# Windowed attention and a three-way maxout layer on one core: the small global transposes are written into the value products' banks

## The chip, the cores and the metric

The kernel runs on one core of a Trainium2 chip. The metric is device time in microseconds (us), from a median of several runs. TensorE (PE in the profile) does the matrix products and writes to PSUM, a memory of eight banks of 128 partitions by 2 KiB (512 numbers of 4 bytes per partition); VectorE (DVE) and ScalarE (ACT) read PSUM and write SBUF; GpSimd (POOL) works in SBUF; SyncE (SP) issues the DMAs.

## The reference

For each of 8 batches and 8 heads there are 512 local and 32 global positions of width 64. A local query sees the 32 global keys and the local keys at a distance of at most 32; a global query sees all keys. The outputs of all heads make a row of 512 numbers for each of the 8 x 544 positions, and each row goes through `max(x@w1, x@w2, x@w3) @ w_out` with widths 512, 768 and 512.

```python
s_ll = np.where(np.abs(pos[:, None] - pos[None, :]) <= 32, scale * q_l @ k_l.T, -1e9)
a_l = sm(np.concatenate([scale * q_l @ k_g.T, s_ll], axis=-1))
out_l = a_l @ np.concatenate([v_g, v_l])
out_g = sm(scale * q_g @ k_all.T) @ v_all
h = np.maximum(np.maximum(x @ w1, x @ w2), x @ w3)
out = h @ w_out
```

## The kernel before

Two heads of a batch make a pair `p` (32 of them). The 512 local queries of a pair are cut in four blocks of 128, and `sl = 4 * p + t` counts these blocks: 128 passes of one loop, called slots here. For each slot:

- `scores(sl)`: products of queries and a window of 192 or 224 keys into an S bank (L313 in the first 28 slots, L317 later; a `pm` bank in the first 12), reduction for the maximum on VectorE (L320), exponential on ScalarE (L322), the reciprocal of the sums (L324, L325) and the scaling (L112). The result goes by DMA into `early` or `prob`.
- `trans(sl)`: four transposes on TensorE into the T bank (L340), copied to the tile `pt`.
- `transg(sl)`: one transpose of 128x128 (L361) of a part of `probg`, which holds the global queries' probabilities. Its result is copied to the columns 128 to 160 of `pt` (hi by `copy`, L102 or L100; the rest by `sub`, L94).
- `pv(sl)`: the product of values and `pt` (L381 in slots 0 to 25, L388 later) into the tile O of two banks, of which it uses columns 0 to 160 of the first bank (early) or 0 to 320 of both (later). Later slots read O four times: a copy of its lower half (lox, L102 or L100), an addition of halves (L394) and two more additions (L396) that give `xr`. Early slots read it once, by a copy to `xr`.
- `glob(p, step)`: the global queries' scores into an S bank (L271, later L275), reduced in L279, for the next pair in the slots with t = 0 and 1; `glob_soft` (L287 to L293) follows with t = 2 and moves the result by six DMAs (L296) to `probg`.

From slot 26 on the operands are split in a rounded part and a rest of it (`copy` and `sub`); `copy`, `sub` and `times` choose their engine by a running sum of costs per engine. The maxout layer of the batch before is a generator of matmuls into `pm` banks (L419 and L438, 512 columns each); `fill(n)` takes n of them and so lays them between the parts of a slot: 18 per slot. In the first part of the program the layer's weights are loaded and converted (L160 to L180) by `weight_step`.

PSUM is used up: three `pm` banks, two for S, one for T, two for O. O is there once, S twice, so an allocation of S waits until the tile two allocations before has been read. The program is written in the order of the loop; a scheduler then sets each engine's order by its own costs and adds the semaphore waits, so the order on an engine is fixed when the kernel is built.

Of the kernel before, what the change touches and what calls it, by code (L numbers as in the profile page):

```python
# [9 lines left out]
F32 = mybir.dt.float32  # L10
# [37 lines left out]
def f32(ap):  # L48
    return ap.bitcast(F32)


def body(ctx, tc, kin, qin, vin, min_, w1, w2, w3, w4, out):
# [8 lines left out]
    psS = ctx.enter_context(tc.tile_pool(name="psS", bufs=2, space=PSUM))  # L61
    psT = ctx.enter_context(tc.tile_pool(name="psT", bufs=1, space=PSUM))
    psO = ctx.enter_context(tc.tile_pool(name="psO", bufs=1, space=PSUM))
# [12 lines left out]
    def spend(e, ns):  # L76
        load[e] += ns
# [11 lines left out]
    def sub(out, a, b, psum=False):  # L89
        n = width(out)  # L90
        c = {"d": n * 1.04 + (160 if psum else 110)}
        if not psum:
            c["p"] = n * 2.32 + 130
        (dve if least(c) == "d" else pool).tensor_tensor(out=out, in0=a, in1=b, op=ALU.subtract)  # L94

    def copy(out, a, psum=False):
        n = width(out)
        c = {"d": n * (1.04 if psum else 0.52) + (160 if psum else 150), "a": n * 0.833 + (150 if psum else 190)}
        if least(c) == "d":
            dve.tensor_copy(out=out, in_=a)  # L100
        else:
            act.copy(out=out, in_=a)  # L102
# [229 lines left out]
    def trans(sl):  # L332
# [15 lines left out]
        else:  # L348
# [2 lines left out]
            copy(v[:, :, 0, 0:128], src, True)  # L351
            sub(v[:, :, 1, 0:128], src, f32(v)[:, :, 0, 0:128], True)

    def transg(sl):
        if sl >= NS:
            return
        p, t = divmod(sl, 4)
        pt = pts[sl]
        i, h, n = GCH[t]
        g = psS.tile([128, 512], F32, name="S")  # L360
        pe.transpose(g.bitcast(F32R)[:, 0:128], probg[p % 2][:, i], identr)  # L361
        src = g[:, 64 * h:64 * h + 64 * n].rearrange("p (c j g) -> p c j g", j=2, g=SG)
        if sl < NAT:
            copy(pt.rearrange("p j c q -> p c j q")[:, 0:n, :, 128:160], src, True)
            return
        v = pt.rearrange("p j c a q -> p c j a q")
        hi, lo = v[:, 0:n, :, 0, 128:160], v[:, 0:n, :, 1, 128:160]
        copy(hi, src, True)
        sub(lo, src, f32(hi), True)

    def pv(sl):
        p, t = divmod(sl, 4)
        pt = pts.pop(sl)
        o = psO.tile([128, 2, 512], F32, name="O")
        if t == 0:
            xr[p] = xp.tile([128, 4, 160], F32, name="xr")
        if sl < NAT:

            for c, j in ((0, 0), (0, 1), (1, 0), (1, 1)):
                n = 160 if c < GCH[t][2] else 128  # L380
                pe.matmul(o[64 * j:64 * j + 64, 0, 0:n], lhsT=vraw[sl][:, 2 * j + c], rhs=pt[:, j, c, 0:n], start=(c == 0), stop=(c == 1))  # L381
            copy(xr[p][:, t], o[:, 0, 0:160], True)
        else:

            for j in range(2):
                for c in range(2):
                    n = 160 if c < GCH[t][2] else 128
                    pe.matmul(o[:, j, 0:320].rearrange("p (a q) -> p a q", a=2)[:, :, 0:n],  # L388
                              lhsT=vs[sl][:, 2 * j + c].rearrange("p a d -> p (a d)"),
                              rhs=pt[:, j, c, :, 0:n], start=(c == 0), stop=(c == 1))  # L390
            lo = att.tile([64, 2, 160], F32, name="lox", bufs=1)
            copy(lo, o[64:128, :, 0:160], True)
            spend("d", 460 + 2 * 320)
            dve.tensor_tensor(out=lo, in0=o[0:64, :, 160:320], in1=lo, op=ALU.add)  # L394
            for j in range(2):
                dve.tensor_tensor(out=xr[p][64 * j:64 * j + 64, t], in0=o[0:64, j, 0:160], in1=lo[:, j], op=ALU.add)  # L396
        if t == 3:
            dve.tensor_reduce(out=xg[:, p % NP, p // NP], in_=xr[p][:, :, 128:160].rearrange("p t g -> p g t"),
                              axis=AX.X, op=ALU.add)
# [101 lines left out]
    load_v(2)  # L501
    weight_load()
    transg(0)
    for sl in range(NS):
        p, t = divmod(sl, 4)
        b, n = divmod(p, NP)
        settle(4500)
        if sl % 16 == 0 and b:
            fill(400)
            mm[0] = moe_local(b - 1)  # L510
        trans(sl + 1)
        fill(4)
        next_scores(max(min(sl + 5, EARLY - 1), sl + 3))
        if t == 2:
            split_k(p + 2)
            load_k(p + 3)
        fill(4)
        pv(sl)
        if t <= 1:
            glob(p + 1, t)  # L520
        elif t == 2:
            glob_soft(p + 1)
        fill(3)
        transg(sl + 1)
        fill(7)
        split_v(sl + 2)
        load_v(sl + 3)
        for _ in range(WS[sl] if sl < len(WS) else 0):
            weight_step()
        if sl % 16 >= 12:  # L530
            i = sl % 16 - 12
            q = b * NP + i
            xs.setdefault(b, []).append(split_x(xr[q][:, :, 0:128], SL))
# [56 lines left out]
```

## Time and profile before

| | |
|---|---|
| time, median of 3 runs | 861.93 us (860.92 to 863.58) |
| time of the profiled execution | 862.75 us |
| its span, first to last instruction | 860.8 us |
| TensorE busy / weight loads | 809.9 / 673.8 us |
| VectorE, ScalarE, GpSimd busy | 577.0, 517.2, 509.9 us |
| granted TensorE clock, mean | 0.977 |
| L361 transposes | 128, median 222 ns |

In rows of the trace the first number is the start in us and the second the duration; `x4` counts merged instructions, and the brackets give idle time of the engine before the row and what ended it. In rows of waits the numbers are total us, times, and the longest. "Behind" a value product means after the end of its last matmul.

### The profile page before, as it was taken

The page shows a single profiled execution, that of the slowest core. Times are in us where ns is not written, and L with a number is a line of the kernel's source. Part 1 is how long each engine was busy: PE and PEld are TensorE (multiplying, and loading weights), DVE is VectorE, ACT ScalarE, POOL GpSimd, SP SyncE. Part 2 cuts the span into 40 slices and gives each one's busy share as a digit, 9 for nine tenths or more (in the row PEclk, how much of TensorE's full clock was granted, in tenths as well). Part 3 has the DMA queues.
Part 4 walks back from the last instruction along what each step waited for, and adds up shares of the span by engine and source line. Part 5 has one row for each costly group of instructions (what it writes and reads, how often), then busy time and mean ns, then how long its engine had stood idle before and what let it go on. Part 6 is the DMA issues. An engine that isn't in the chain of part 4 may idle for free.

```text
span 860.8 us, 15729 instructions
## 1 busy us (share of the span) xinstructions
PE 809.9 (94%) x4452; PEld 673.8 (78%) x4452; DVE 577.0 (67%) x1806; ACT 517.2 (60%) x1457; POOL 509.9 (59%) x683
## 2 busy tenths in 40 slices
PE   5857888899999999999999999999999999999997
PEld 3534565688888888888888888888888888888896
DVE  5567999677777677776777777867787776511111
ACT  4654554587677667767777777776777776511111
POOL 4535676686667666776768576766677664411211
PEclk8886999999999999999999999999999999999999
DMA  6685664435333533344333533353334322100001
GB/s 211 188 245 162 195 197 146 137 95 156 99 106 102 160 112 107 99 126 127 100 110 100 150 98 103 92 163 108 111 112 131 123 79 67 62 24 1 26 25 25
DMA packets 107238, 98.53 MB, mean 114 GB/s; under 512 B 21008, under 2 KB 97936, under 8 KB 107152
## 3 DMA queue, kind: packets, MB, share of 16 engines
q1 hardware_dynamic: 107152, 97.53, 37.5%
q8 instruction: 36, 0.59, 0.3%
q14 instruction: 50, 0.41, 0.1%
HBM read 56.85 MB, written 8.91 MB: 76 GB/s over the span
## 4 chain that ended last, share of the span: by engine, by line
PE 83%; DVE 7%; DMA 5%; SPq 2%; issue 2%; ACT 1%; POOL 1%; DVEq 0%; ACTq 0%; POOLq 0%
PE pm L419 46%; PE pm L438 17%; PE O L388 7%; PE S L317 5%; PE T L340 4%; DVE wraw L170 2%; PE S L275 1%; DMA wraw<-w_in 1%; DMA probg<-sg 1%; DMA prob<-s 1%; DVE cut L171 1%; PE S L361 1%; PE pm L313 1%; SPq L296 1%; DMA early<-s 1%
## 5 line engine op out<-in xcount | busy, mean ns | idle before, releaser
L419 PE MATMUL pm<-xs,wh 128*128 128x512 f32 (+1 forms) x1296 | 408.9, 389 | 1.4 <-POOL xs L94 0.9
L419 PEld LDWEIGHTS pm<-xs,wh 128*128 128x128 f32 x1296 | 234.1, 190 | 34.3 <-POOL xs L94 1.2
L419 PE MATMUL pm<-xs,wl 128*128 128x512 f32 (+1 forms) x648 | 253.5, 391 | 0.0
L112 POOL TENSOR_SCALAR s<-s,z 128x192 f32<-128x192 f32 (+1 forms) x249 | 113.4, 468 | 86.4 <-ACT lox L102 36.8
L322 ACT ACTIVATE s<-s,nm 128x192 f32<-128x192 f32 (+1 forms) x256 | 118.1, 462 | 40.1 <-DVE nm L320 35.3
L419 PEld LDWEIGHTS pm<-xs,wl 128*128 128x128 f32 x648 | 122.9, 190 | 22.5 <-issue 1.8
L438 PE MATMUL pm<-woh,h 128*128 128x512 f32 x408 | 133.5, 398 | 0.0
L94 POOL TENSOR_TENSOR h<-m,h 128x512 fp32r<-128x512 f32 (+1 forms) x54 | 67.5, 1250 | 96.2 <-ACT h L102 96.1
L427 DVE TENSOR_TENSOR m<-pm,m 128x512 f32<-128x512 f32 (+1 forms) x108 | 71.1, 658 | 71.7 <-PE pm L419 71.4
L94 POOL TENSOR_TENSOR qs<-qraw,qs 128x256 fp32r<-128x256 f32 x100 | 73.9, 749 | 54.9 <-ACT qs L102 41.2
L94 DVE TENSOR_TENSOR pt<-T,pt 128x512 fp32r<-128x512 f32 x102 | 70.5, 691 | 49.3 <-ACT pt L102 47.4
L324 DVE TENSOR_SCALAR z<-z 128x2 f32<-128x2 f32 x128 | 55.0, 430 | 50.9 <-ACT s L322 50.2
L320 DVE CUSTOM_DVE_ANT_0 s<-S,mask 128x192 f32<-128x192 f32 (+1 forms) x232 | 78.1, 370 | 11.9 <-PE S L313 5.6
L438 PEld LDWEIGHTS pm<-woh,h 128*128 128x128 f32 x408 | 74.7, 188 | 11.5
L438 PE MATMUL pm<-wol,h 128*128 128x512 f32 x204 | 81.8, 401 | 0.0
L94 POOL TENSOR_TENSOR vs<-vraw,vs 128x256 fp32r<-128x256 f32 x102 | 75.6, 741 | 10.0 <-ACT vs L102 6.5
L94 POOL TENSOR_TENSOR kst<-kraw,kst 64x576 fp32r<-64x576 f32 x50 | 71.9, 1439 | 11.8 <-issue 8.3
L102 ACT CAST pt<-T 128x512 fp32r<-128x512 f32 x91 | 53.2, 585 | 40.2 <-PE T L340 39.9
L388 PEld LDWEIGHTS O<-pt,vs 128*128 128x128 f32 x408 | 66.5, 188 | 9.1
L388 PE MATMUL O<-pt,vs 128*128 128x320 f32 (+1 forms) x408 | 72.8, 300 | 0.0
L102 ACT CAST qs<-qraw 128x256 fp32r<-128x256 f32 x100 | 40.7, 407 | 49.8 <-PE S L317 48.1
L340 PEld LDWEIGHTS T<-identr,prob 128*128 128x128 f32 x448 | 50.3, 141 | 22.3 <-ACT s L322 2.6
(93 smaller groups left out, 1282.4 us busy)
## 6 DMA issues: line engine op xcount, KB each, us to landing
vraw<-v_in SPq DMA_DIRECT2D x128, 128.0 KB, 2.5
qraw<-q_in SPq DMA_DIRECT2D x100, 128.0 KB, 2.2
prob<-s SPq DMA_DIRECT2D x56, 224.0 KB, 2.4
prob<-s SPq DMA_DIRECT2D x56, 192.0 KB, 2.3
wraw<-w_in SPq DMA_DIRECT2D x18, 512.0 KB, 5.1
out_dram<-o SPq DMA_DIRECT2D x32, 256.0 KB, 2.5
kraw<-k_in SPq DMA_DIRECT2D x25, 320.0 KB, 3.1
qn<-q_in SPq DMA_DIRECT2D x28, 128.0 KB, 3.7
```

What stands on the lines that cost most here:

```text
L94: (dve if least(c) == "d" else pool).tensor_tensor(out=out, in0=a, in1=b, op=ALU.subtract)
L102: act.copy(out=out, in_=a)
L112: pool.tensor_scalar(out=out, in0=a, scalar1=col, scalar2=1.0, op0=ALU.mult, op1=ALU.mult)
L317: pe.matmul(ph[j][:, 0:n], lhsT=qs[sl][:, a, 128 * j:128 * j + 128], rhs=kst[p][:, j, c0:c0 + n], start=(a == 0), stop=(a == 1))
L320: dve.tensor_tensor_reduce(out=s[:, j, 0:n], in0=ph[j][:, 0:n], in1=mask[:, (1, 0, 1, 0)[t], 32 * (t == 0):32 * (t == 0) + n], scale=-0.12 ...
L322: act.activation(out=s[:, j, 0:n], in_=s[:, j, 0:n], func=AF.Exp, bias=nm[:, j:j + 1], scale=-1.0, accum_out=z[:, j:j + 1])
L324: dve.tensor_scalar(out=z, in0=z, scalar1=1e-9, scalar2=None, op0=ALU.add)
L340: i = pe.transpose(pr[:, 256 * j + 128 * c:256 * j + 128 * c + 128], s[:, j, 128 * c:128 * c + 128], identr)
L388: pe.matmul(o[:, j, 0:320].rearrange("p (a q) -> p a q", a=2)[:, :, 0:n], lhsT=vs[sl][:, 2 * j + c].rearrange("p a d -> p (a d)"), rhs=pt[ ...
L419: pe.matmul(ps[:, 0:n], lhsT=w[f][:, i, k], rhs=xs[k][:, a, 0:n], start=(q == 0), stop=(q == 11))
L427: dve.tensor_tensor(out=m[:, 0:n], in0=ps[:, 0:n], in1=m[:, 0:n], op=ALU.max)
L438: pe.matmul(ps, lhsT=hh[f][:, a, 128 * t:128 * t + 128], rhs=w[:, f], start=(q == 0), stop=(q == 17))
```

## The change

`transg` no longer allocates an S tile. It writes its 128 columns into columns 384 to 512 of the second bank of the O tile that the last `pv` used (a first one is allocated for slot 0). `pv` puts its new tile in the list `obank`. The S banks are left to `scores` and `glob`. Line numbers behind `transg` rise by 5: L361 becomes L366, L388 L393, L394 L399, L396 L401, L419 L424.

```diff
+    obank = [None]
+
     def transg(sl):
...
         i, h, n = GCH[t]
-        g = psS.tile([128, 512], F32, name="S")
+
+        if obank[0] is None:
+            obank[0] = psO.tile([128, 2, 512], F32, name="O")
+        g = obank[0][:, 1, 384:512]
         pe.transpose(g.bitcast(F32R)[:, 0:128], probg[p % 2][:, i], identr)
...
     def pv(sl):
         p, t = divmod(sl, 4)
         pt = pts.pop(sl)
-        o = psO.tile([128, 2, 512], F32, name="O")
+        o = obank[0] = psO.tile([128, 2, 512], F32, name="O")
```

TensorE in a slot with t = 0 in the middle of the program, before, from the last value product on (`pm` rows are fillers, the numbers behind names tell tiles apart):

```order
L388 MATMUL O_6215<-pt_6104,vs_6091 128x2x128
L275 MATMUL S_6229<-kst_6042,qgz_96 128x384 [waits PE_49]
L275 MATMUL S_6229<-kst_6042,qgz_96 128x384
L419 MATMUL pm_6184<-xs_6096,wl0_108 128x512
L419 MATMUL pm_6184<-xs_6171,wh0_102 128x512 [waits Activation_49]
L419 MATMUL pm_6184<-xs_6171,wh0_102 128x512 [waits Pool_49]
L361 MATMUL S_6237<-identr_87,probg0_94 128x128 [waits DMAHW3_49,DMAHW2_49,DVE_49]
L419 MATMUL pm_6184<-xs_6171,wl0_108 128x512
```

The same place after:

```order
L393 MATMUL O_6135<-pt_6025,vs_6012 128x2x128
L275 MATMUL S_6149<-kst_5964,qgz_96 128x384 x2
L424 MATMUL pm_6104<-xs_6017,wl0_108 128x512
L424 MATMUL pm_6104<-xs_6091,wh0_102 128x512
L424 MATMUL pm_6104<-xs_6091,wh0_102 128x512 [waits Pool_49]
L424 MATMUL pm_6104<-xs_6091,wl0_108 128x512
L424 MATMUL pm_6162<-xs_5846,wh0_102 128x512 x2
L424 MATMUL pm_6162<-xs_5846,wl0_108 128x512
L366 MATMUL O_6135<-identr_87,probg0_94 128x128 [waits DMAHW2_49,DMAHW3_49,DVE_49,Activation_49]
```

The transpose stood behind three fillers and waited for VectorE's reading of an S tile. It stands behind seven now, writes the tile of the value product just ahead of it (O_6135), and waits for VectorE and ScalarE; the score product L275 has lost its wait. The VectorE instruction that it waits for is the second L401 of that tile. With t = 2 and 3, where no L275 is in between, it comes behind eight fillers. No filler is added or dropped.

VectorE in the next slot (t = 1), before, from the addition on O:

```order
L394 TENSOR_TENSOR lox_6300<-O_6295,lox_6300 64x320 [waits Activation_49]
L279 ISA sg_6226,nmg_6227<-S_6305,sg_6226 64x160 [waits Activation_49]
L279 ISA nmg_6227 64x1
L396 TENSOR_TENSOR xr_6216<-O_6295,lox_6300 64x160 [waits DVE_49]
L396 TENSOR_TENSOR xr_6216<-O_6295,lox_6300 64x160
L94 TENSOR_TENSOR pt_6260<-S_6313,pt_6260 128x2x32 [waits Activation_49]
L287 TENSOR_TENSOR nmg_6227<-nmg_6227 64x1 [waits DVE_49]
L427 TENSOR_TENSOR m_6183<-pm_6292,m_6183 128x512 [waits PE_49]
```

The same place after:

```order
L399 TENSOR_TENSOR lox_6219<-O_6214,lox_6219 64x320 [waits Activation_49]
L279 ISA sg_6146,nmg_6147<-S_6224,sg_6146 64x160 [waits Activation_49]
L279 ISA nmg_6147 64x1
L401 TENSOR_TENSOR xr_6136<-O_6214,lox_6219 64x160 [waits DVE_49]
L401 TENSOR_TENSOR xr_6136<-O_6214,lox_6219 64x160
L287 TENSOR_TENSOR nmg_6147<-nmg_6147 64x1 [waits DVE_49]
L289 TENSOR_SCALAR zg_6148<-zg_6148 64x1 [waits Activation_49]
L94 TENSOR_TENSOR pt_6179<-O_6214,pt_6179 128x2x32 [waits Activation_49]
L432 TENSOR_TENSOR m_6103<-pm_6211,m_6103 128x512 [waits PE_49]
```

The subtraction that reads the transposed block (`pt` from S, now from O) went behind L287, and L289, which waits for ScalarE's exponential, now stands ahead of it and of the maximum (L427, now L432). The additions on O and the reduction L279 between them keep their places.

TensorE near the program's start, before, from the second slot's transposes on:

```order
L340 MATMUL T_242<-identr_87,early_114 128x128 [waits DMAHW2_49,Activation_49]
L340 MATMUL T_242<-identr_87,early_114 128x128 x3
L361 MATMUL S_239<-identr_87,probg0_94 128x128 [waits DMAHW6_49,DMAHW3_49]
L271 MATMUL S_293<-kn_130 64x384
L381 MATMUL O_283<-pt_233,vraw_128 64x160 [waits Activation_49]
L381 MATMUL O_283<-pt_233,vraw_128 64x160
L381 MATMUL O_283<-pt_233,vraw_128 64x128 x2
L361 MATMUL S_296<-identr_87,probg0_94 128x128 [waits DMAHW5_49,DMAHW4_49,PE_49]
```

After, from the third slot's scores on:

```order
L313 MATMUL pm_190<-kn_118,qn_126 128x224 [waits DMAHW4_49]
L313 MATMUL pm_190<-kn_118,qn_126 128x224
L271 MATMUL S_293<-kn_130 64x384 [waits DMAHW6_49,DVE_49]
L313 MATMUL pm_207<-kn_118,qn_132 128x192 [waits DMAHW7_49,DVE_49]
L313 MATMUL pm_207<-kn_118,qn_132 128x192
L313 MATMUL pm_249<-kn_130,qn_149 128x192 [waits DMAHW0_49,DVE_49]
L313 MATMUL pm_249<-kn_130,qn_149 128x192
L313 MATMUL pm_266<-kn_130,qn_166 128x224 [waits DMAHW1_49,DVE_49]
```

The second pair's first global scores (S_293) stood behind the first transpose of `probg`; they now stand ahead of the scores of the fourth slot.

## The prediction

> **What bounds the kernel now.** I read the page's engine line and its slices first, then busy time by stage, then who TensorE waits for, and last the single slots (a slot is one pass of the loop over `sl`).
>
> ```profile
> span 860.8 us, 15729 instructions
> PE 809.9 (94%) x4452; PEld 673.8 (78%) x4452; DVE 577.0 (67%) x1806; ACT 517.2 (60%) x1457; POOL 509.9 (59%) x683
> PE   5857888899999999999999999999999999999997
> ```
>
> TensorE is the bound as a whole, with two regimes: partly idle in the first eight slices (about 170 us), full after that.
>
> ```profile
> core 0: us, PE busy (x) PEld busy (x) DVE busy (x) ACT busy (x) POOL busy (x), PEclk, DMA share, GB/s
> 80.00:100.00 20.00, 15.19 (x86) 10.65 (x87) 19.82 (x54) 10.64 (x33) 13.94 (x12) 1.00 0.68 199
> 120.00:140.00 20.00, 17.36 (x90) 12.53 (x91) 19.76 (x41) 11.15 (x29) 13.48 (x14) 0.95 0.67 194
> 400.00:500.00 100.00, 100.00 (x555) 84.85 (x554) 74.96 (x244) 71.45 (x201) 69.20 (x97) 1.00 0.38 114
> ...
> PE S L361 <- DMA probg<-sg: 14.1, 4, 4.4
> PE S L361 <- DVE nm L320: 6.2, 5, 2.2
> ...
> PE S L361 <- DVE nm L320: 2.2, 1, 2.2
> PE T L340 <- DMA prob<-s: 0.4, 1, 0.4
> ```
>
> The windows show VectorE as the early limit from 80 to 140 us (19.8 of 20) and a TensorE without any idle time from 200 us on (100.00 of 100). The first two wait rows are of the whole run; the last two are all that TensorE waits for between 165 and 760 us. So what the change takes away, the global transpose's (L361) wait for a score bank still being read (released by L320), is 6.2 us in five waits, and only 2.2 us of it lies in the full stretch. In that stretch every new wait of TensorE goes straight onto the end: the filling matmuls are issued in a fixed order behind it.
>
> **The change part by part.** The same instructions run on every engine; only the bank of 128 transposes and the order move.
>
> *Removed: waits for an S bank.* At most 6.2 us; surely on the path is the single 2.2 us at the start of the full stretch. The others lie where VectorE or DMAs set the pace. I take 3 us.
>
> *Moved early: the global scores.* In the new order the second pair's global scores (L271) stand before its local scores and no longer behind the first global transpose. They are two short matmuls beside idle TensorE time. VectorE's reduction that follows stands at nearly its old place, and the four waits for `probg` (14.1 us) hang on the DMAs behind it. I take nothing; the ends are -14.1 us (all go) and +5 us (shuffled weight conversions on the VectorE-bound stretch, about the 6.2 us row turned round).
>
> *Added: the transpose waits for the value product's readers.* From slot 26 on, `pv` leaves two banks that are read by a copy (lox), L394 and twice L396. The transpose of the next slot now writes into the second of these banks, and the new program makes it wait for the second L396. To cover this wait the scheduler put the transpose 8 filling matmuls behind `pv` (7 and the global scores where t is 0 or 1), where before it came after 3. Is that far enough? One slot of each t, first TensorE's rows, then VectorE's:
>
> ```profile
> 496.09 0.69 PE L388 MATMUL O<-pt,vs 128*128 128x320 f32 x4
> 497.31 0.22 PE L361 MATMUL S<-identr,probg 128*128 128x128 f32 x1
> 498.06 0.65 DVE L396 TENSOR_TENSOR xr<-O,lox 64x160 f32<-64x160 f32 x2
> ...
> 501.68 0.74 PE L388 MATMUL O<-pt,vs 128*128 128x320 f32 x4
> 502.96 0.22 PE L361 MATMUL S<-identr,probg 128*128 128x128 f32 x1
> 503.54 0.23 DVE L94 TENSOR_TENSOR pt<-S,pt 128x64 fp32r<-128x64 f32 x1
> 503.68 0.64 DVE L396 TENSOR_TENSOR xr<-O,lox 64x160 f32<-64x160 f32 x2
> ...
> 507.35 0.69 PE L388 MATMUL O<-pt,vs 128*128 128x320 f32 x4
> 508.23 0.40 PE L419 MATMUL pm<-xs,wl 128*128 128x512 f32 x1
> 508.46 0.62 PE L419 MATMUL pm<-xs,wh 128*128 128x512 f32 x2
> 508.92 0.22 PE L361 MATMUL S<-identr,probg 128*128 128x128 f32 x1
> 508.98 0.45 PE L419 MATMUL pm<-xs,wl 128*128 128x512 f32 x1
> 509.26 0.63 PE L419 MATMUL pm<-xs,wh 128*128 128x512 f32 x2
> 509.89 0.65 DVE L396 TENSOR_TENSOR xr<-O,lox 64x160 f32<-64x160 f32 x2
> ...
> 513.32 0.74 PE L388 MATMUL O<-pt,vs 128*128 128x320 f32 x4
> 514.82 0.22 PE L361 MATMUL S<-identr,probg 128*128 128x128 f32 x1
> 515.30 0.64 DVE L396 TENSOR_TENSOR xr<-O,lox 64x160 f32<-64x160 f32 x2
> ```
>
> Filling matmuls start 0.23 us apart (508.23, 508.46). So the transpose's new place is its old start plus 5 x 0.23 = 1.15 us in the first two slots (t = 2, 3) and plus 4 x 0.23 = 0.92 us in the others (t = 0, 1): 498.46, 504.11, 509.84, 515.74. The second L396 ends at 498.71, 504.32, 510.54, 515.94: later in all four. In the second slot the subtraction `pt<-S` (L94) stood ahead of L396 and took 0.14 us of its time (503.54 to 503.68); it now comes behind, so 504.18 there.
>
> What a late release costs TensorE is seen where a transpose did wait for VectorE:
>
> ```profile
> 133.87 0.08 DVE L320 DVE_READ_ACCUMULATOR2_ANT nm<- 128x1 f32 x1
> 134.01 0.14 PEld L361 LDWEIGHTS S<-identr,probg 128*128 128x128 f32 x1 [2.17 <-DVE nm L320]
> 134.12 0.46 PE L419 MATMUL pm<-xs,wl 128*128 128x512 f32 x1
> 134.42 0.62 PE L419 MATMUL pm<-xs,wh 128*128 128x512 f32 x2
> ```
>
> The release is at 133.95, the second matmul behind the transpose starts at 134.42, 0.47 us later; without a wait (508.92 to 509.26) it is 0.34 us behind the transpose's own start. The delay is therefore release minus place plus 0.13 us: 0.38 (t=2), 0.20 (t=3), 0.83 (t=0), 0.33 (t=1), together 1.74 us in four slots. There are 101 such transposes, about 25 sets of four: 43.5 us as the upper bound.
>
> The lower bound asks how early the readers can be done if nothing is queued before them:
>
> ```profile
> L396 DVE TENSOR_TENSOR xr<-O,lox x204: 303/317/320, 175.9 to 755.8; 64x160 f32<-64x160 f32 x102
> L394 DVE TENSOR_TENSOR lox<-O,lox x102: 460/481/485, 175.4 to 754.9; 64x320 f32<-64x320 f32 x102
> L102 ACT COPY lox<-O x97: 422/423/425, 174.6 to 754.5; 64x320 f32<-64x320 f32 x97
> ```
>
> 0.42 + 0.48 + 2 x 0.32 = 1.54 us, with three or four handovers of 0.03 about 1.65 us behind the end of `pv`. The place lies 1.68 us behind it (498.46 less the 496.09 + 0.69 of its row) for t = 2 and 3, and 1.80 us (509.84 less 507.35 + 0.69) for t = 0. That leaves 0.10, 0.10 and 0. For t = 1 a reduction of the global scores stays between L394 and L396 in both orders, so its 0.33 stays. 0.53 x 25 = 13 us. Between 13 and 43.5 I take 36, near the upper end, because what makes the readers late is set off behind the transpose of the slot before, and so isn't given a lead by that one's delay: in the t = 0 slot a small VectorE instruction stands still until a long GpSimd one is through,
>
> ```profile
> 508.21 1.07 DVE L324 TENSOR_SCALAR z<-z 128x2 f32<-128x2 f32 x1 [0.95 <-ACT s L322]
> 507.81 1.44 POOL L94 TENSOR_TENSOR kst<-kraw,kst 64x576 fp32r<-64x576 f32 x1
> ```
>
> and GpSimd's order is the same in both programs in this stretch. A few us less than the bound, since ScalarE and VectorE have some more idle time per slot.
>
> The trace of before has no TensorE write beside a read of the same bank, so no row prices it. The Trainium skill ("PSUM — Partial Sum Buffer", PSUM bank collisions raise a hardware error) says that a TensorE write and a VectorE read of one bank and the same partitions collide even at disjoint columns, so that a guard must go by bank. By that rule the free columns are no free place, and the sum is the one above; were columns enough, the wait would be unneeded and the sum would be the removed waits alone, 859.
>
> *The transposed blocks' way to the next value product.* It now starts about 1.1 us later, on ScalarE (copy, L102) and VectorE (L94). Behind it 11 filling matmuls, four transposes and four scores still stand before the next `pv`, over 3 us; I cost it at nothing, covered by these. In slots with t = 1 the cover is thinnest (third rival).
>
> *Slots below 26.* The transpose waits for ScalarE's copy of the product (L102 xr). TensorE has idle time there; nothing.
>
> **Sum.** +36 - 3 = +33 us on the profiled execution's 862.75 us (span 860.8), so 895.8; the median of the runs is 861.93, 0.8 less, hence 895.
>
> **The rivals.** *TensorE swallows the delays: no change.* The windows row has weight loads at 84.85 of 100 us. The Trainium skill ("Perfetto Trace Analysis", Identifying the Most-Contended Engine) says that matmul busy time overstates how near TensorE is to its limit and that weight-load time is the better measure; by it 15% would be free, more than the 7% that 0.4 us of a slot of 5.7 us takes. Then the time would be 862 less 3, or 859 to 862. Against it: after the wait at 134 us the matmuls follow at the usual 0.23 us (134.12 and 134.42 even further apart), nothing is caught up. 5%.
>
> *Faster: the early global scores pay.* If the four `probg` waits (14.1) and all S waits (6.2) went and the full stretch lost its 13 us alone: 862 - 20 + 13 = 855. It decides from an early gain above the loss in the slots, so above 13 us at least. Against it, VectorE at 19.8 of 20 us from 80 to 140 us. 8%.
>
> *Slower still: `pv` waits too.* With t = 1 VectorE now holds L289, waiting for the exponential of the global scores, ahead of the subtractions that `pv` needs. If that made `pv` late by 0.5 us in 25 slots: +12 us, 905 to 909. 12%.
>
> **How the numbers follow.** The forecast, delays of 0.1 to 0.8 us in each slot, has 75%: 862 + 13 - 6 = 869 to 862 + 43.5 + 3 = 908. The range for 8 in 10 takes the forecast's bounds and half of the third rival: 868 to 909. No change is within 0.3% (2.6 us), about what a measurement of this kernel tells apart. Slower 75 + 12 = 87%, same 5%, faster 8%.
>
> **What would show it.** Right: TensorE's waits list a new first group, the transpose released by L396's successor (L401 xr), some 100 times, 20 to 45 us, the longest where t = 0; TensorE's busy share in the hundreds of us falls from 100 to about 93; a slot takes 6.0 to 6.1 us instead of 5.7. Right for the early part: no wait of the transpose for L320. Wrong: TensorE still full from 200 to 700 us, or the start of the full stretch more than 5 us from 167 us.

## The result and the profile after

The changed kernel takes 902.67 us (901.65 to 904.51 in four runs) against 862.42 us (860.92 to 863.58): 1.0469 times the time before, with an interval of 1.0453 to 1.0485. It is 40 us slower. Its profiled execution has a span of 899.5 us, 38.7 us more than before. The head of its page, three windows of it, and rows of what TensorE waits for (the first two of the whole run, the last four between 165 and 800 us; each row gives total us, times and the longest):

```profile
span 899.5 us, 15800 instructions
PE 832.3 (93%) x4452; PEld 671.1 (75%) x4452; DVE 578.9 (64%) x1806; ACT 524.1 (58%) x1457; POOL 511.6 (57%) x683
PE   5868888899999999999999999999999999999997
```

```profile
core 0: us, PE busy (x) PEld busy (x) DVE busy (x) ACT busy (x) POOL busy (x), PEclk, DMA share, GB/s
80.00:100.00 20.00, 17.95 (x94) 12.48 (x93) 19.48 (x49) 10.15 (x30) 12.93 (x14) 0.94 0.59 177
120.00:140.00 20.00, 18.91 (x106) 14.26 (x105) 19.43 (x38) 9.98 (x27) 13.13 (x13) 1.00 0.63 205
400.00:500.00 100.00, 95.90 (x516) 77.81 (x514) 70.21 (x228) 67.65 (x189) 65.47 (x91) 1.00 0.35 107
```

```profile
PE O L366 <- DMA probg<-sg: 6.6, 4, 3.1
PE O L366 <- ACT xr L102: 6.0, 8, 1.5
...
PE O L366 <- issue: 9.9, 23, 1.3
PE O L366 <- ACT m L102: 9.6, 12, 2.7
PE O L366 <- DVE xr L401: 4.8, 24, 0.2
PE O L366 <- ACT kst L102: 2.1, 7, 0.7
```

The slices say little: a 9 stays a 9. The stretch from 400 to 500 us shows the loss: TensorE starts 516 matmuls there instead of 555, and loads weights for 77.81 us instead of 84.85. The last four rows are all that the waits list in the full stretch. They belong to the transpose, now L366. Together they are only 26.4 us, and three of the four name something other than the reader of O. The single transposes show which it was. One slot of each t (2, 3, 0, 1), TensorE's rows and those of VectorE and GpSimd that matter:

```profile
516.03 0.69 PE L393 MATMUL O<-pt,vs 128*128 128x320 f32 x4
518.05 0.65 DVE L401 TENSOR_TENSOR xr<-O,lox 64x160 f32<-64x160 f32 x2
518.80 0.25 PE L366 MATMUL O<-identr,probg 128*128 128x128 f32 x1 [0.27 <-issue]
...
522.09 0.74 PE L393 MATMUL O<-pt,vs 128*128 128x320 f32 x4
523.92 0.65 DVE L401 TENSOR_TENSOR xr<-O,lox 64x160 f32<-64x160 f32 x2
524.67 0.25 PE L366 MATMUL O<-identr,probg 128*128 128x128 f32 x1
...
527.95 0.69 PE L393 MATMUL O<-pt,vs 128*128 128x320 f32 x4
528.40 1.44 POOL L94 TENSOR_TENSOR kst<-kraw,kst 64x576 fp32r<-64x576 f32 x1
528.80 1.06 DVE L324 TENSOR_SCALAR z<-z 128x2 f32<-128x2 f32 x1 [0.95 <-ACT s L322]
530.48 0.65 DVE L401 TENSOR_TENSOR xr<-O,lox 64x160 f32<-64x160 f32 x2
531.23 0.25 PE L366 MATMUL O<-identr,probg 128*128 128x128 f32 x1 [0.64 <-ACT m L102]
...
534.77 0.74 PE L393 MATMUL O<-pt,vs 128*128 128x320 f32 x4
536.75 0.64 DVE L401 TENSOR_TENSOR xr<-O,lox 64x160 f32<-64x160 f32 x2
537.54 0.25 PE L366 MATMUL O<-identr,probg 128*128 128x128 f32 x1 [0.20 <-DVE xr L401]
```

The second L401 ends at 518.70, 524.57, 531.13 and 537.39, and the transpose starts 0.10, 0.10, 0.10 and 0.15 us later, whatever the bracket names. The bracket puts a wait for several semaphores down to one of them. In the t = 3 slot there is no bracket at all, although the transpose is held there as well. It is so in the whole stretch: each of the 101 transposes behind the first of these products starts 0.06 to 0.15 us after the end of the second L401, in slot 26 too, where the row on `m` with 2.7 us lies.

The time splits at the first value product in its later form (L393, before L388). One row of each kernel grouped by form has its shortest, middle and longest duration in ns and its first and last start in us:

```profile
L388 PE MATMUL O<-pt,vs x408: 278/306/311, 171.7 to 754.1; 128*128 128x320 f32 x102, 128*128 128x256 f32 x34
```

```profile
L393 PE MATMUL O<-pt,vs x408: 278/305/310, 167.2 to 792.8; 128*128 128x320 f32 x102, 128*128 128x256 f32 x34
```

The first 26 slots are over 4.5 us earlier (171.7 to 167.2). The stretch from the first to the last of these products grew from 582.4 to 625.6 us, by 43.2. What follows the last is as long as before (106.7 us). 43.2 - 4.5 = 38.7, the difference of the spans. These starts come from one profiled execution of each kernel, while the runs of one kernel differ by about 3 us or more, so a us or two between two first products means little.

### The profile page after: what moved, and what is told of

The parts are those of the page before. It is cut to its first block, busy times and chain, and to the rows that moved or that the text cites. A ratio compares the mean times of both kernels' runs of the same rounds, so it can differ in the third digit from the quotient of the medians.

```text
span 899.5 us, 15800 instructions
## 1 busy us (share of the span) xinstructions
PE 832.3 (93%) x4452; PEld 671.1 (75%) x4452; DVE 578.9 (64%) x1806; ACT 524.1 (58%) x1457; POOL 511.6 (57%) x683
## 4 chain that ended last, share of the span: by engine, by line
PE 72%; DVE 9%; ACT 7%; DMA 6%; issue 4%; POOL 1%; SPq 1%; ACTq 0%; DVEq 0%; POOLq 0%
PE pm L424 39%; PE pm L443 14%; PE O L393 5%; PE S L317 5%; PE T L340 4%; PE O L366 3%; DMA wraw<-w_in 2%; DVE xr L401 2%; ACT s L322 1%; DVE wraw L170 1%; DVE lox L399 1%; DMA early<-s 1%; ACT lox L102 1%; ACT kst L102 1%; DVE sg L279 1%
## 5 line engine op out<-in xcount | busy, mean ns | idle before, releaser
L424 PE MATMUL pm<-xs,wh 128*128 128x512 f32 (+1 forms) x1296 | 420.1, 392 | 0.0
L424 PEld LDWEIGHTS pm<-xs,wh 128*128 128x128 f32 x1296 | 231.4, 190 | 30.5 <-issue 0.4
L424 PE MATMUL pm<-xs,wl 128*128 128x512 f32 (+1 forms) x648 | 249.4, 385 | 0.0
L112 POOL TENSOR_SCALAR s<-s,z 128x192 f32<-128x192 f32 (+1 forms) x249 | 115.2, 475 | 86.8 <-ACT lox L102 42.0
L443 PE MATMUL pm<-woh,h 128*128 128x512 f32 x408 | 136.7, 401 | 0.0
L424 PEld LDWEIGHTS pm<-xs,wl 128*128 128x128 f32 x648 | 122.9, 190 | 17.0 <-issue 1.4
L432 DVE TENSOR_TENSOR m<-pm,m 128x512 f32<-128x512 f32 (+1 forms) x108 | 70.9, 657 | 62.1 <-PE pm L424 61.4
L320 DVE CUSTOM_DVE_ANT_0 s<-S,mask 128x192 f32<-128x192 f32 (+1 forms) x232 | 78.0, 371 | 13.7 <-PE S L313 6.9
L324 DVE TENSOR_SCALAR z<-z 128x2 f32<-128x2 f32 x128 | 52.0, 406 | 53.9 <-ACT s L322 53.5
L366 PEld LDWEIGHTS O<-identr,probg 128*128 128x128 f32 x128 | 18.5, 145 | 81.3 <-issue 33.0
L393 PEld LDWEIGHTS O<-pt,vs 128*128 128x128 f32 x408 | 66.4, 188 | 9.0
L393 PE MATMUL O<-pt,vs 128*128 128x320 f32 (+1 forms) x408 | 72.7, 299 | 0.0
L366 PE MATMUL O<-identr,probg 128*128 128x128 f32 x128 | 34.4, 269 | 39.0 <-issue 9.9
```

The costliest lines, as they stand in the source:

```text
L112: pool.tensor_scalar(out=out, in0=a, scalar1=col, scalar2=1.0, op0=ALU.mult, op1=ALU.mult)
L320: dve.tensor_tensor_reduce(out=s[:, j, 0:n], in0=ph[j][:, 0:n], in1=mask[:, (1, 0, 1, 0)[t], 32 * (t == 0):32 * (t == 0) + n], scale=-0.12 ...
L324: dve.tensor_scalar(out=z, in0=z, scalar1=1e-9, scalar2=None, op0=ALU.add)
L424: pe.matmul(ps[:, 0:n], lhsT=w[f][:, i, k], rhs=xs[k][:, a, 0:n], start=(q == 0), stop=(q == 11))
L432: dve.tensor_tensor(out=m[:, 0:n], in0=ps[:, 0:n], in1=m[:, 0:n], op=ALU.max)
L443: pe.matmul(ps, lhsT=hh[f][:, a, 128 * t:128 * t + 128], rhs=w[:, f], start=(q == 0), stop=(q == 17))
```

## The experiments

My theory was that TensorE loses the time in the stretch from slot 26 on, because the second L396 (now L401) ends behind the transpose's place; rivals were a loss elsewhere (early slots, the order of VectorE, the value product) and a loss that no wait makes. All kernels are read by two numbers, taken as above from the row of the value product: the start of the first one, and the stretch from the first to the last. The ratios are against runs of the kernel before on the same chip. Slot times are averages over the stretch, from one value product to the next.

| kernel | time us | ratio (95%) | first product | stretch |
|---|---|---|---|---|
| before | 862.42 | | 171.7 | 582.4 |
| after | 902.67 | 1.0469 (1.0453 to 1.0485) | 167.2 | 625.6 |
| early_only | 859.73 | 0.9981 (0.9971 to 0.9992) | 168.1 | 583.2 |
| late_only | 903.17 | 1.0489 (1.0473 to 1.0505) | 170.5 | 622.6 |
| after_no_eps | 879.13 | 1.0211 (1.0196 to 1.0226) | 165.0 | 605.1 |
| before_no_eps | 856.88 | 0.9947 (0.9929 to 0.9966) | 163.3 | 584.3 |
| ten_fill | 872.73 | 1.0137 (1.0119 to 1.0156) | 167.7 | 595.2 |
| ten_fill_no_eps | 855.34 | 0.9926 (0.9901 to 0.9952) | 165.0 | 580.9 |
| early_no_eps | 857.21 | 0.9945 (0.9927 to 0.9963) | 165.4 | 584.4 |
| pm_early | 859.38 | 0.9975 (0.9958 to 0.9992) | 167.8 | 583.6 |
| ten_S | 856.12 | 0.9935 (0.9920 to 0.9949) | 167.1 | 579.2 |
| ten_S_no_eps | 854.04 | 0.9914 (0.9894 to 0.9935) | 168.8 | 576.6 |
| ten_early_no_eps | 854.42 | 0.9904 (0.9879 to 0.9930) | 165.0 | 578.2 |

### Each half of the change alone

`early_only` and `late_only` choose the bank by the slot; NAT is 26.

```diff
+        if sl < NAT:
...
             g = obank[0][:, 1, 384:512]
+        else:
+            g = psS.tile([128, 512], F32, name="S")
```

`late_only` has `sl >= NAT` in its place and needs no first O tile.

> The transpose goes to the O tile in slots 0 to 25 alone and to an S bank from slot 26 on, as before. My theory: the change has two independent parts. The early one let the first split-form value product start at 167.2 us instead of 171.7 us, a gain of 4.5 us; the late one costs 43.2 us over 101 slots. So this kernel: 862.4 - 4.5 = 858 us (856 to 860), full stretch without waits of TensorE. Rival: the 4.5 us is an accident of the changed order on VectorE (weight conversions) that comes with any new order; then 860 to 865 us.

> The transpose goes to the O tile from slot 26 on and to an S bank before, the other half of the change. My theory: 862.4 + 43.2 = 905.6 us (903 to 908), the same per-slot delays as in the whole change (0.78, 0.35, 0.41, 0.08 us for t = 0, 1, 2, 3), 3 us more than the whole change. Rival, the halves are not independent (the late delays depend on what the early order left queued): more than 4 us away from 905.6.

The early half alone makes the kernel 1.6 us faster (0.9981), less than the 4.5 us that I had read from two first products, and its full stretch is full again: this is its window, 555 matmuls as in the kernel before.

```profile
400.00:500.00 100.00, 100.00 (x555) 84.85 (x554) 74.82 (x245) 71.50 (x203) 68.88 (x96) 1.00 0.37 114
```

The late half alone carries the whole loss: 1.0489, a stretch of 622.6 us. Against the whole change its first product is 3.3 us later and its stretch 3.0 us shorter. Nearly all of the latter is one wait of 2.7 us at 172.4 us (the longest of the L366 row on `m`), in slot 26: there the second reader of O ends 4.41 us behind the product in the whole change and 1.81 us in this kernel. So in these two profiles the whole change gives back at once, where the early slots meet the later ones, most of what it won ahead. The two halves don't add up, and the expected 905.6 was a little too much.

### The readers earlier: L324 out

The longest delay, t = 0, was put down to L324, which stands still beside GpSimd's long subtraction and holds L399 and L401 behind it. L324 adds 1e-9 to a sum that has 1 as one of its terms (the exponential at the maximum), which in numbers of 4 bytes changes nothing; two kernels leave that addition out, one from the changed kernel, one from the kernel before as a control.

```diff
-        dve.tensor_scalar(out=z, in0=z, scalar1=1e-9, scalar2=None, op0=ALU.add)
```

> The whole change without the addition of 1e-9 to the sums (L324), 128 small VectorE instructions; the rest of the computation is the same. My theory: in t = 0 slots this instruction stands still for GpSimd's long subtraction and holds the additions on O behind it; without it the reciprocal (0.17 us) comes at once, the readers end about 1.7 us behind the value product in t = 0 and t = 2, and the delay falls from 0.78 to about 0.05 us and from 0.41 to 0.15 us: 25 x 0.73 + 26 x 0.26 = 25 us less, 878 us (872 to 885). Rival: another VectorE instruction takes over the standing still (the reciprocal or an addition with two inputs), or ScalarE's copy of O is what is late: 895 us or more.

> The kernel before without the addition of 1e-9 to the sums (L324); a control for the run of the whole change without it. My theory: the kernel before has no wait of TensorE in the full stretch, so the addition's standing still costs nothing there and the 23 us that its removal saved in the changed kernel were the waits' alone; only VectorE's early limit gains, 1 to 4 us: 858 to 862 us. Rival: the removal is worth 10 us or more by itself (VectorE's time, fewer instructions), then 852 us or less and the earlier run says less about the waits.

The changed kernel without it takes 879.13, as expected. Its stretch is 20.5 us shorter than the changed kernel's (605.1 to 625.6), while the control's stretch is 1.9 us longer than before (584.3 to 582.4). What the control gains, 4.9 us in its runs, lies ahead of the first product (163.3). So those 20 us were the transpose's wait (about 2 of them in slot 26, where L324 itself took only 0.21 us), and L324 costs TensorE nothing in another way in this stretch. The t = 0 slot of after_no_eps (L324 is the reciprocal here, the lines below it one less):

```profile
513.32 0.69 PE L392 MATMUL O<-pt,vs 128*128 128x320 f32 x4
513.77 1.43 POOL L94 TENSOR_TENSOR kst<-kraw,kst 64x576 fp32r<-64x576 f32 x1
514.16 0.17 DVE L324 RECIPROCAL z<-z 128x2 f32<-128x2 f32 x1 [0.95 <-ACT s L322]
515.13 0.65 DVE L400 TENSOR_TENSOR xr<-O,lox 64x160 f32<-64x160 f32 x2
515.88 0.25 PE L365 MATMUL O<-identr,probg 128*128 128x128 f32 x1
```

GpSimd's subtraction is still there, but the reciprocal runs beside it in 0.17 us. The readers are done 1.77 us behind the product (515.78 less 514.01) where they took 2.49 (531.13 less 528.64), and the transpose starts 0.72 us sooner behind it (1.87 instead of 2.59). A t = 0 slot takes 6.10 us instead of 6.65, t = 2 5.81 instead of 6.05; t = 1 (6.25) and t = 3 (5.80), where L324 does not stand in the way, stay as they were.

### The transpose later: ten fillers ahead of it

```diff
-        fill(3)
+        fill(10)
         transg(sl + 1)
-        fill(7)
```

> The whole change, but the transpose is written behind ten fillers instead of three and stands behind ten on TensorE in every slot from 26 on. The readers of O are untouched. My theory, the cost is the place against the end of the readers: the place moves to 2.14 us (t = 2, 3), 2.49 (t = 0) and 2.37 us (t = 1) behind the value product; with the readers' ends of the whole change (1.99, 1.66, 2.48, 1.88 us) and the 0.13 us of a wait only t = 0 is still late, by 0.1 to 0.6 us, some 5 us in all: 862.4 - 4.5 + 6 = 864 us (860 to 869). Rival: writing beside the value product costs something that does not depend on the place (the bank, the shared tile, ScalarE's and VectorE's order): 890 us or more. Second rival: the blocks now come too late for the next value product, 8 fillers on: waits of O (L393) for VectorE's pt, 0.3 us or more a slot, 880 us or more.

872.73 us, above the expected 860 to 869: the place behind more fillers takes away 30 of the 43 us of the stretch (595.2). In slots with t = 1 and t = 3 no delay is left (5.82 and 5.63 us, shorter than the 5.87 and 5.70 of before), and t = 0 keeps the 0.2 us that were expected (6.14 us, 5.93 before). But t = 2 takes 5.97 (5.56 before), and here is why:

```profile
451.40 1.29 POOL L94 TENSOR_TENSOR h<-m,h 128x512 fp32r<-128x512 f32 x1
451.73 0.68 PE L393 MATMUL O<-pt,vs 128*128 128x320 f32 x4
452.55 0.86 DVE L324 TENSOR_SCALAR z<-z 128x2 f32<-128x2 f32 x1 [0.80 <-ACT s L322]
452.65 0.74 POOL L94 TENSOR_TENSOR qs<-qraw,qs 128x256 fp32r<-128x256 f32 x1
454.03 0.65 DVE L401 TENSOR_TENSOR xr<-O,lox 64x160 f32<-64x160 f32 x2
454.78 0.25 PE L366 MATMUL O<-identr,probg 128*128 128x128 f32 x1
```

L324 now stands still for 0.86 us until the subtraction `qs` ends, where it took 0.48 in such a slot of the kernel before:

```profile
496.69 0.73 POOL L94 TENSOR_TENSOR qs<-qraw,qs 128x256 fp32r<-128x256 f32 x1
496.97 0.48 DVE L324 TENSOR_SCALAR z<-z 128x2 f32<-128x2 f32 x1 [0.80 <-ACT s L322]
```

So the second L401 ends 2.27 us behind the product (454.68 less 452.41) instead of 1.98 in the changed kernel. The later place was partly overtaken by later readers. A single wait of 3.4 us of the value product for `pt` comes on top:

```profile
PE O L393 <- DVE pt L94: 3.4, 1, 3.4
```

I had taken the readers' time as fixed against the product, and in this order it isn't: `qs` starts 0.24 us behind the product's end here (452.65 less 452.41) and 0.09 us ahead of it in the slot of before (496.69, with the end at 496.78). Both edits together test that:

> The whole change with the transpose behind ten fillers and without the addition of 1e-9. My theory: with the place at 2.14 to 2.49 us and the readers done at 1.7 to 2.0 us no transpose waits any more (t = 2 with its 0.4 us a slot was the same standing still behind GpSimd as t = 0), and the time is that of the early gain alone: 856 to 861 us. Rival: a part of the 10 us that ten fillers left over is another cost of the shared tile: 866 us or more.

855.34 us, 0.7 us below the range that was expected: with readers early and place late the stretch is 580.9 us, 1.5 shorter than before. In it the transpose waits once:

```profile
PE O L392 <- DVE pt L94: 3.1, 1, 3.1
PE O L365 <- DVE xr L400: 1.0, 1, 1.0
```

So the new bank costs nothing by itself; its price is the wait, and the wait is the distance between place and readers. The last runs below hold the check of it: `ten_S_no_eps` differs from this kernel in the transposes' bank alone, its time can't be told apart (0.9914 and 0.9926, with intervals that overlap), and the median slot of each kind takes the same within 0.01 us in both.

### Where the early gain comes from

`pm_early` is the kernel before but for the bank of the transposes in the first 16 slots, one of the `pm` banks, which also leaves S to the scores.

```diff
-        g = psS.tile([128, 512], F32, name="S")
+        g = pm.tile([128, 512], F32, name="pm") if sl < 16 else psS.tile([128, 512], F32, name="S")
```

> The kernel before with the transposes of slots 0 to 15 written into a pm bank, S banks from slot 16 on: the early S banks are freed as in the change, but without the wait for the copy of the value product. My theory: the early gain comes from the freed S banks (the next pair's global scores no longer queue behind the transposes), so it shows here too, 857 to 861 us. Rival: the gain of the early half is an accident of the new order; this other new order then gives anything between 860 and 868 us.

859.38 us (0.9975, where early_only has 0.9981), the first product at 167.8: the same gain by another bank, which speaks for the freed S banks without showing them as the cause. `early_no_eps` (the edits of early_only and before_no_eps together) asks whether this gain and the control's add up:

> The transpose in the O tile in slots 0 to 25 alone, and no addition of 1e-9. My theory: both gains lie in the first 170 us and add in part: 1.6 us (early half alone) and 2 us (less VectorE work where it is the limit), 857 to 860 us, the fastest so far. Rival: the early stretch is set by the weights' DMAs and by luck of the order; within 0.3% of the kernel before, and not faster than the early half alone.

They don't: 857.21 us is what the control alone has (856.88), and its first product is later than the control's (165.4 to 163.3).

### Is there something in the place alone

That ten_fill's t = 1 and t = 3 slots were shorter than before suggested that the place is worth something whatever the bank. `ten_S` is the kernel before, with S banks, and ten fillers ahead of the transpose (the same diff of `fill` as above).

> The kernel before (transposes in S banks) with the transpose behind ten fillers, next to the four transposes of L340. The slots of the run with ten fillers in the O tile and without the addition of 1e-9 were 0.05 to 0.06 us shorter on average than those with the transpose alone between fillers (t = 0: 5.87 against 5.93, t = 1: 5.82 against 5.87, t = 3: 5.63 against 5.70). My theory: a lone transpose between 512-column matmuls costs TensorE about 0.05 us more than one beside other transposes, whatever bank it writes; 101 x 0.05 = 5 us: 861.7 - 5 = 857 us (855 to 859). Rival: the shorter slots came from the O tile or from the missing addition: 861 to 863 us. Second rival: scores wait for S banks now, since the transpose's tile is held next to them: 865 us or more.

856.12 us (0.9935), within the expected 855 to 859, but not all by the reason given: the profile has 3.2 us less in the stretch, where 5 were expected, and 4.6 less ahead of it, where nothing was; what made the first product earlier wasn't traced. A t = 0 slot's transpose in it, beside the four of L340, and below it the four of L340 of the kernel before, without it:

```profile
504.43 0.39 PE L419 MATMUL pm<-xs,wl 128*128 128x512 f32 x1
504.66 0.22 PE L361 MATMUL S<-identr,probg 128*128 128x128 f32 x1
504.72 0.48 PE L340 MATMUL T<-identr,prob 128*128 128x128 f32 x4
505.03 0.70 PE L419 MATMUL pm<-xs,wh 128*128 128x512 f32 x2
```

```profile
510.65 0.45 PE L340 MATMUL T<-identr,prob 128*128 128x128 f32 x4
510.95 0.70 PE L419 MATMUL pm<-xs,wh 128*128 128x512 f32 x2
```

Five transposes in a row take 0.37 us until the next filler starts (504.66 to 505.03), four 0.30 (510.65 to 510.95): the fifth costs 0.07 there. Alone between fillers, as in the kernel before, it costs 0.11 (508.46 to 509.26 for three fillers and the transpose, less 3 x 0.23). 101 x 0.04 = 4 us, about the 3.2 that the stretch became shorter; most single slots in it became 0.03 to 0.07 us shorter. Last come the two versions that put the pieces together: ten_S without the addition, and ten_S without it and with the early transposes in O:

> The same without the addition of 1e-9. My theory: both gains add, 856.9 - 5 = 852 us (850 to 854), which beats the O tile with ten fillers and no addition (855.3) by the one wait of 3.1 us that it still had. Rival: no better than 855 us, when the shorter slots belong to the O tile.

> O tile in slots 0 to 25, S banks from 26 on, ten fillers, no addition of 1e-9: every gain seen, without the late waits. My theory: 857.2 - 5 = 852 us (850 to 855); the early O tile adds nothing to what the missing addition gives early, as without ten fillers (857.2 against 856.9). Rival: the early gain adds after all, below 850 us.

854.04 and 854.42 us (0.9914 and 0.9904) can't be told apart, and neither reached the 852 that was expected from adding up the gains. Both beat the kernel before by nearly 1% and the changed one by 5%. The late transposes are in S in both.

## Why the prediction was right, and where its sizes were off

*The late transposes' wait: the mechanism right, the size 7 us too small.* The term was 36 us, and the stretch grew by 43.2. The four delays that I read from the trace of before were 0.38, 0.20, 0.83 and 0.33 us (t = 2, 3, 0, 1); the slots grew by 0.49, 0.11, 0.72 and 0.39 us on average, 1.71 for 1.74 in all. That four slots came so near was luck in part: slots of one kind differ (with t = 0 they grew by 0.01 to 1.38 us), and 2.88 us of the growth are slot 26 alone, with its wait of 2.7 us, which no sampled slot stood for. The same working (release less place plus 0.13 us, with the 0.14 us of t = 3) on all 101 slots of the trace of before gives 45.0 us (12.8, 3.0, 20.1 and 9.0 by kind, where 12.8, 2.7, 18.0 and 9.7 came). In slot 26 of that trace the second reader already ended 4.12 us behind the product. So the step that failed is the choice below the bound: I gave the readers a few us for idle time in a longer slot. They used little of it. Behind the product the second reader ends 1.98, 1.74, 2.49 and 1.88 us in the four slots shown above, and in those of before 1.93, 1.90, 2.50 and 1.88. A longer slot moves the product and its readers together, because the copy and the additions start from the product, and what stands in their way, GpSimd's subtraction, keeps its place beside it. The one reading that did shift is t = 3, by 0.16 us, for the 0.14 of the subtraction that went behind L396.

*The transpose waits although its columns are free.* The new program waits for L401 although the transpose writes columns that L401 doesn't read, and the runs show that this wait is the price. The second L401 reads the very bank that the transpose writes, so no run tells a guard by bank from one by the whole tile. No run leaves the guard out, so whether columns of one bank could do without it wasn't tried. The Trainium skill ("PSUM — Partial Sum Buffer", PSUM bank collisions raise a hardware error) rules it out.

*Removed and early: -3 taken, -4.5 between the two profiles, -1.6 by the runs of early_only.* No row of the transpose's waits names L320 any more. The waits for `probg` fell from 14.1 to 6.6 us, and TensorE does more in the windows from 80 to 100 and from 120 to 140 us (17.95 and 18.91 of 20, for 15.19 and 17.36), while VectorE is busy 0.3 us less in each. What I costed at nothing, the early transpose's wait for the copy `xr`, is there with 6.0 us in eight waits. That the rest is the freed S banks is supported by pm_early and not settled: ten_S keeps the S banks in use and starts its first product at 167.1, so other orders of the same work gain as much.

*The rival of a TensorE with room to spare* fell: weight loads left 15% of the time free, and yet every delay came through, since the fillers stand behind the held transpose in one queue. The Trainium skill ("Perfetto Trace Analysis", Identifying the Most-Contended Engine) names weight loads the better measure of this engine. For the size of the loss the trace agrees: per 100 us, loading time fell by 8.3% (84.85 to 77.81) and the count of matmuls by 7.0% (555 to 516), near the 6.9% that 582.4 is below 625.6, while busy time fell by 4.1%. As a sign of room in which a wait costs nothing it misled here. That busy time by itself overstates shows between 400 and 500 us: it is 100.00 of 100 us with 555 matmuls before, and 100.00 with 562 in ten_S_no_eps.

*The rival of a value product that waits as well* did not come: none of the rows of its waits lies in the full stretch. It came once each in ten_fill (3.4 us) and ten_fill_no_eps (3.1). *The rival of an early gain above the loss* fell too, with at most 4.5 us against 43.2.

*The signs.* I named 100 waits of 20 to 45 us put down to L401. The sum of the rows is 26.4 us, but only 24 of the 66 waits in them carry that name, and 43.2 - 26.4 = 17 us of the loss are in no row. They lie under the filler ahead of the transpose: it is recorded with 0.39 us, though the next one could start 0.23 us after it, so the first 0.16 us of each hold don't show as idle, 16 us in 101 slots. The matmuls themselves are hardly longer (their durations in the stretch add up to 1106.2 us, for 1103.5); they overlap less. So TensorE's busy time rose from 809.9 to 832.3 us with the same 4452 matmuls, and the busy share fell to 96 and not to 93. Slots take 6.19 us on average, a little above the 6.0 to 6.1 that followed from 36 us.

## What to carry to other kernels

Columns that were free in a bank weren't free in time: the transpose put there waited for the last reader of the tile. Before moving work like this, take the readers' end and the new place, both counted from the instruction that filled the bank, out of every slot if the rows are there: the sum of their differences over 101 slots was right to 4% (45.0 and 43.2 us), one slot of each kind came as near partly by luck, and a discount for slack made it worse. If the place is too early, the wait can be worked on from both ends, but only both together took it away here, and the bank that was used before, with the better place alone, was as good.

## What the runs showed of the hardware that was not expected

- A VectorE addition on 128x2 numbers (L324) takes 0.17 us where no GpSimd instruction runs (the row below, from the t = 3 slot of the changed kernel), but 1.06 us when a GpSimd subtraction is running as it starts, and it ends with that one (529.86 and 529.84 us in the slot with t = 0 above). The reciprocal of the same 128x2 numbers in its place runs through. The Trainium skill ("SBUF — State Buffer", Who interferes with whom) says that a `tensor_scalar` can take a mode in which it and a GpSimd instruction shut each other out for the whole instruction; the trace agrees as far as VectorE's waiting goes, and doesn't show the mode. In ten_fill the addition stood through two: it started at 452.55, ahead of the subtraction `qs` (452.65), while the one before was still running, and ended at 453.41 with `qs` (453.39).

```profile
522.95 0.17 DVE L324 TENSOR_SCALAR z<-z 128x2 f32<-128x2 f32 x1 [0.20 <-ACT s L322]
```

- A single transpose between wide matmuls costs about 0.04 us more than one beside other transposes (0.11 and 0.07 us, each read at one place), an estimate from these rows that the slots of ten_S, mostly 0.03 to 0.07 us shorter, bear out.
- Idle time in the trace is less than the time lost by short waits on TensorE: 26.4 of 43.2 us here, because a matmul is recorded past the point at which the next could start (0.39 and 0.23 us). The count of matmuls per 100 us shows all of it (7.0%, for 6.9% of the stretch).
